# Fifteen tiny loads of 1 to 15 rows, issued between the second and the third piece of the last weight load

## The chip, the cores and the metric

The kernel runs on one core of a Trainium2 chip. The metric is the device time of one execution in microseconds (us); the number that counts is the median over several runs.

## What is computed

One token is decoded through an attention layer with a long cache, a gated feed-forward layer, and a gate that mixes the two:

```python
q = x @ wq                                   # 32 query heads of 128
scores = einsum(q, k) * Dh ** -0.5           # 8 key heads, each for 4 query heads, 32768 positions
p = softmax(scores)
a = einsum(p, v).reshape(B, Sq, Hq * Dh) @ wo    # wo is 4096 x 512
b = (silu(x @ w1) * (x @ w3)) @ w2           # 512 -> 1792 -> 512
g = sigmoid((x * gate_w).sum(-1))
out = g * a + (1 - g) * b
```

All data is float32. Keys and values make up most of what has to be read from memory: 8 x 32768 x 128 numbers each.

## The kernel before

The whole program is written as a list of operations per engine. A small planner (the class `Program`) goes through them in the order of the code, notes who writes and who reads what, and puts the semaphore waits in; each engine then runs its own list in that order. So the order of the code is the order on each engine.

SyncE (SP in the profile) issues all big loads, on one queue (q1 in the profile). `load` (L199) issues one, with a semaphore for that load. Two large buffers, `big_a` and `big_b`, of 128 rows by 16384 numbers each take turns: keys in 8 MB pieces, the query weights first, the values in 8 MB pieces. A load into a buffer waits, on SyncE, for the last reader of what lies in it. TensorE takes the products; VectorE turns the keys; ScalarE copies and takes the exponentials.

At the end stands the part that the change touches. The last four value pieces are loaded by `load_unit` (L199) and used by `values` (TensorE, L574). Behind the last value piece SyncE issues `w2` into the tile `aside`, and then, as soon as TensorE has read the first part of head 7 out of `big_a`, the output weights `wo` into the same buffer, in six pieces whose sizes fall from 4096 KB to 256 KB:

```python
    parts = ((0, 16), (16, 23), (23, 27), (27, 29), (29, 31), (31, 32))
    for a, b in parts:
        load(wo_t[:, a:b, :], wod[:, a:b, :], [("wo", a)], over=["A0", "A1"])
```

Each piece is 128 rows; piece (a, b) has 2048 bytes times (b - a) in a row. TensorE multiplies the first three pieces at L630 (27 slices of 512 columns) and the last three at L661 (in 128 columns each), each when its piece has landed. VectorE then copies the result (L673), SyncE and ScalarE each store half of it (L504), and GpSimd waits for the two stores at the very end.

The tile `kt1`, into which the change loads, is 2048 numbers wide. In its first 1024 columns lies `otp`, the turned attention output that the last products read; the other 1024 columns are not read any more by then.

Of the kernel before, what the change touches and what calls it, by code (L numbers as in the profile page):

```python
# [118 lines left out]
def kernel(  # L119
# [13 lines left out]
    nc = tc.nc  # L133
# [23 lines left out]
    pr = Program(nc, tc.alloc_semaphore)  # L157
# [5 lines left out]
    def sbuf(name, *shape):  # L163
        return nc.alloc_sbuf_tensor(name, [P, *shape], F32)[:]
# [4 lines left out]
    kt = [pool_w[:, NB * 96:NB * 128], sbuf("kt1", NB * 32)]  # L169
# [25 lines left out]
    def load(dst, src, writes, over=()):  # L195
        lanes[0] += 1
        lane = f"load{lanes[0] % 9}"
        return pr.add(
            "SP", lambda: nc.sync.dma_start(dst, src), writes=writes, over=[*over, lane], inc=lane, by=16, also=lane,  # L199
        )  # L200
# [60 lines left out]
    def zeros():  # L261
        return T.matmul(ps_s, acc[:, 0:P], acc, start=True, stop=False, skip_group_check=True)  # L262
# [344 lines left out]
    wod = wo.rearrange("(p k) e -> p k e", k=32)  # L607
    parts = ((0, 16), (16, 23), (23, 27), (27, 29), (29, 31), (31, 32))
    for a, b in parts:
        load(wo_t[:, a:b, :], wod[:, a:b, :], [("wo", a)], over=["A0", "A1"])  # L610


    def spend(bank, n):
# [68 lines left out]
    a, b, c, d = flips  # L682
# [24 lines left out]
    with nc.Fori(0, NH - LAG, 1, engines=[PE], head_slot={PE: 0}):  # L707
# [8 lines left out]
        values_all().then_inc(done, 1)  # L716
        zeros().then_inc(done, 1)
    pr.emit("PE", ops[d:])
    landed = pr.semaphore("stored")
    nc.gpsimd.wait_ge(landed, 32).then_inc(landed, 1)  # L720
    critical.close()
# [28 lines left out]
```

## Time and profile before

| | |
|---|---|
| median of 3 runs | 693.91 us |
| lowest and highest run | 693.82 and 694.04 us |
| profiled execution, from its first to its last instruction | 692.4 us |
| TensorE busy | 402.8 us (58%) |
| VectorE busy | 368.4 us (53%) |
| ScalarE busy | 134.6 us (19%) |
| time of the packets on the load queue, as a share of 16 DMA engines | 99.1% |
| read from memory | 296.23 MB, 428 GB/s over the span |

The profiled execution is known by its span alone: 692.4 us lie between its first and its last instruction. The time of a run is counted from outside, and the median is 1.5 us longer than that span. The engines are a little over half busy at most; the DMA engines, which carry the loads, are busy nearly all the time.

### The profile page before, as it was taken

The numbers are of one execution on the slowest core, as the hardware profiler recorded it, in microseconds if no ns is written. First come the engines' busy times: TensorE is split into PE (matmuls) and PEld (weight loads), VectorE is DVE, ScalarE is ACT, GpSimd is POOL, SyncE is SP. The second block draws the span as 40 slices with busy tenths as digits, with TensorE's granted clock in tenths as the row PEclk, the third lists the DMA queues.
The fourth block names the chain that finished last, engine by engine and source line by source line (L and its number), as shares of the span: only waits on it lengthen the run. The fifth ranks groups of instructions, "written<-read, shape, count | busy, mean of one in ns | idle before, by whom it ended". The sixth has DMA issues, their size and how long they took to land. (4 is left out here: it accounts for less than half of the span.)

```text
span 692.4 us, 5704 instructions
## 1 busy us (share of the span) xinstructions
PE 402.8 (58%) x2430; PEld 94.6 (14%) x2430; DVE 368.4 (53%) x229; ACT 134.6 (19%) x113; POOL 8.1 (1%) x34
## 2 busy tenths in 40 slices
PE   1537777566474656557484645666573646744575
PEld 0101111201010110201010101201010102211121
DVE  0049999394735637493726537593826546700026
ACT  0143223232303130220303131210303131100000
POOL 4000000000000000000000000000000000000000
PEclk9969999958667676977786777778586777776689
DMA  9999999999999999999999999999999999999996
GB/s 386 455 428 424 424 424 436 448 443 424 428 428 428 435 454 432 424 432 428 432 454 435 424 428 428 432 435 451 432 424 428 428 435 454 435 421 424 433 421 284
DMA packets 6068, 296.34 MB, mean 428 GB/s; under 512 B 678, under 2 KB 682, under 8 KB 1068
## 3 DMA queue, kind: packets, MB, share of 16 engines
q1 hardware_dynamic: 6052, 296.23, 99.1%
q8 instruction: 5, 0.08, 0.0%
q14 instruction: 3, 0.02, 0.0%
q10 hardware_dynamic: 8, 0.01, 0.0%
HBM read 296.23 MB, written 0.00 MB: 428 GB/s over the span
## 5 line engine op out<-in xcount | busy, mean ns | idle before, releaser
L366 DVE STREAM_TRANSPOSE aside<-big_a 128x2048 f32<-128x2048 f32 x41 | 94.3, 2300 | 166.9 <-DMA big_a<-in_A_k_cache_dram 166.9
L350 PE MATMUL ps<-aside,winc 128*32 128x512 f32 x512 | 96.0, 830 | 142.4 <-PEq L688 141.5
L350 PE MATMUL ps<-kt,winc 128*32 128x512 f32 x512 | 96.2, 832 | 61.2 <-PEq L688 61.2
L451 PE MATMUL ps<-big_b,pv 128*32 128x512 f32 x768 | 96.1, 657 | 17.5 <-PEq L688 17.5
L338 ACT COPY aside<-big_a 128x6144 f32<-128x6144 f32 x14 | 74.4, 5313 | 151.8 <-DMA big_a<-in_A_k_cache_dram 151.8
L366 DVE STREAM_TRANSPOSE kt<-aside 128x2048 f32<-128x2048 f32 x32 | 73.4, 2293 | 17.2 <-PE ps L350 17.2
L366 DVE STREAM_TRANSPOSE kt<-big_a 128x2048 f32<-128x2048 f32 x28 | 63.5, 2269 | 0.0
L379 ACT COPY sb<-ps 128x512 f32<-128x512 f32 x16 | 17.1, 1069 | 156.8 <-PE ps L350 156.8
L350 PEld LDWEIGHTS ps<-aside,winc 128*32 128x32 f32 x512 | 13.4, 125 | 215.7 <-issue 215.7
L451 PEld LDWEIGHTS ps<-big_b,pv 128*32 128x32 f32 x768 | 27.7, 120 | 88.1 <-issue 88.1
L366 DVE STREAM_TRANSPOSE aside<-aside 128x2048 f32<-128x2048 f32 x16 | 36.3, 2269 | 0.0
L583 DVE TENSOR_TENSOR sb<-ps,own_b 128x512 f32<-128x512 f32 x2 | 1.4, 691 | 60.8 <-PE ps L574 60.8
L350 PEld LDWEIGHTS ps<-kt,winc 128*32 128x32 f32 x512 | 13.3, 123 | 143.8 <-issue 143.8
L574 PE MATMUL ps<-big_b,probs 128*32 128x512 f32 x128 | 18.0, 726 | 18.8 <-DMA big_b<-in_A_v_cache_dram 18.8
L344 ACT COPY winc<-win 128x128 f32<-128x128 f32 x32 | 9.8, 306 | 78.7 <-PE ps L350 78.7
L574 PE MATMUL ps<-big_a,probs 128*32 128x512 f32 x128 | 17.3, 703 | 10.1 <-DMA big_a<-in_A_v_cache_dram 10.1
L614 PE MATMUL ps<-win,ones 128*128 128x512 f32 x42 | 22.7, 635 | 0.0
L366 DVE STREAM_TRANSPOSE aside<-big_b 128x2048 f32<-128x2048 f32 x7 | 16.0, 2291 | 11.4 <-DMA big_b<-in_A_k_cache_dram 11.4
L262 PE MATMUL ps<-acc 128*128 128x512 f32 x34 | 20.0, 670 | 2.5 <-POOL acc L219 1.6
L400 DVE TENSOR_REDUCE mt<-turned 128x8 f32<-128x2048 f32 x4 | 9.2, 2291 | 22.6 <-PE turned L389 22.6
L424 DVE TENSOR_REDUCE sums<-probs 128x8 f32<-128x2048 f32 x4 | 15.2, 3801 | 2.1 <-ACT probs L417 2.1
L288 PE MATMUL turned<-big_a,xp 128*32 128x512 f32 x64 | 8.5, 691 | 12.1 <-DMA big_a<-in_A_wq_dram 12.1
(93 smaller groups left out, 186.6 us busy)
## 6 DMA issues: line engine op xcount, KB each, us to landing
big_b<-in_B_w_dram SPq DMA_DIRECT2D x2, 3584.0 KB, 20.8
big_a<-in_A_wo_dram SPq DMA_DIRECT2D x1, 4096.0 KB, 27.6
aside<-in_B_w_dram SPq DMA_DIRECT2D x1, 3584.0 KB, 37.4
big_a<-in_A_wo_dram SPq DMA_DIRECT2D x1, 1792.0 KB, 31.5
big_a<-in_A_wo_dram SPq DMA_DIRECT2D x1, 1024.0 KB, 33.5
big_a<-in_A_wo_dram SPq DMA_DIRECT2D x2, 512.0 KB, 34.7
big_a<-in_A_wo_dram SPq DMA_DIRECT2D x1, 256.0 KB, 35.2
big_a<-in_A_k_cache_dram SPq DMA_DIRECT2D x14, 26.3
```

Of the source, the lines that this page charges most:

```text
L262: return T.matmul(ps_s, acc[:, 0:P], acc, start=True, stop=False, skip_group_check=True)
L288: ins = T.matmul(pf[b][32 * j:32 * j + 32, :], xp[:, c, :], t[:, o:o + REP * DH], start=(c == 0), stop=(c == NC - 1),)
L338: act(lambda: A.copy(spare, src[:, :, 32:128]), reads=[key], writes=["wo"])
L344: lambda: A.copy(winc, win[:, t // 4, :, 16 - 16 * z:48 - 16 * z]),
L350: ins = T.matmul(ps_s[32 * g:32 * g + 32, :], winc[:, c, :], kt[c % 2][:, 512 * g:512 * g + 512], start=False, stop=False, skip_group_chec ...
L366: k = dve(lambda d=dst, s=src: V.transpose(d, s), reads=[key], writes=[f"kt{c % 2}"], over=["kt0"] * (t >= LAG and (z, c) == (1, 1)), cred ...
L379: lambda: A.copy(sb[:, :, :, t % 4], ps_s.rearrange("p (n i) -> p n i", i=32)),
L400: dve(lambda: V.tensor_reduce(mt[:, 0:8], turned.rearrange("p (n q) -> p q n", q=8), axis=AX.X, op=ALU.max), reads=banks, writes=["mt"])
L424: dve(lambda: V.tensor_reduce(sums[:, 8 * w:8 * w + 8].rearrange("p (u q) -> p u q", u=2), probs[:, :, 0:1024].rearrange("p u (n q) -> p u ...
L451: ins = T.matmul(ps_o[32 * t:32 * t + 32, :], pv[:, o:o + 32], big[1][:, n * P:(n + 4) * P], start=((z, g) == (0, 0)), stop=((z, g) == (1, ...
L574: ins = T.matmul(ps_o[32 * t:32 * t + 32, :], prob[u][:, o:o + 32], vt[:, n * P:(n + 4) * P], start=((e, z, g) == (0, 0, 0)), stop=((e, z, ...
L614: return T.matmul(bank[:, 0:n], ones, win.rearrange("p w c n -> p (w c n)")[:, 0:n], start=True, stop=True)
```

## The change

Between the second and the third piece of `wo`, SyncE issues fifteen more loads. Load n has n rows (n from 1 to 15) of 4 + n numbers (20 to 76 bytes), from the start of the first n rows of the `wo` view, into the unused columns of `kt1`. They all count up one semaphore, `few`, by 16 each. No engine reads what they bring. GpSimd waits for `few` to reach 240, ahead of its last wait.

```diff
     for a, b in parts:
         load(wo_t[:, a:b, :], wod[:, a:b, :], [("wo", a)], over=["A0", "A1"])
+        for n in range(1, 16) if a == 16 else ():
+            pr.add("SP", lambda n=n: nc.sync.dma_start(kt[1][0:n, 1024 + 32 * n:1028 + 33 * n], wod[0:n, 0, 0:4 + n]),
+                   writes=[("few", n)], over=["kt1"], inc="few", by=16)
...
     pr.emit("PE", ops[d:])
+    nc.gpsimd.wait_ge(pr.semaphore("few"), 15 * 16)
     landed = pr.semaphore("stored")
     nc.gpsimd.wait_ge(landed, 32).then_inc(landed, 1)
```

This is what stands on SyncE in the changed kernel around the place, with each instruction's waits (the rows L199 are pieces of `wo`, the rows L612 the new loads into `kt1`):

```order
L199 DMA big_a<-in_A_wo_dram 128x8192 [waits PE]
L199 DMA big_a<-in_A_wo_dram 128x3584
L612 DMA kt<-in_A_wo_dram 1x5
L612 DMA kt<-in_A_wo_dram 2x6
...
L612 DMA kt<-in_A_wo_dram 14x18
L612 DMA kt<-in_A_wo_dram 15x19
L199 DMA big_a<-in_A_wo_dram 128x2048
L199 DMA big_a<-in_A_wo_dram 128x1024 x2
L199 DMA big_a<-in_A_wo_dram 128x512
L504 DMA out_dram<-winc 2x128 [waits DVE]
```

The four last pieces of `wo` have moved behind fifteen issues; the new loads wait for nothing themselves. On GpSimd the difference is in one row, at the end of the program, behind the last tile that it clears:

```order
 L536 MEMSET kt 128x1024 [waits PE]
 L199 UNCONDITIONAL_BRANCH
-L156 UNCONDITIONAL_BRANCH [waits stored]
+L156 UNCONDITIONAL_BRANCH [waits stored,few]
 L156 NO_OP [waits Activation_49]
```

One wait has come in beside the one on the stores; nothing else has moved there.

## Rows read from the trace of the kernel before

**Rows 1.** The page: DMA busy tenths in 40 slices, and the queues (packets, MB, share).

```profile
DMA  9999999999999999999999999999999999999996
q1 hardware_dynamic: 6052, 296.23, 99.1%
q10 hardware_dynamic: 8, 0.01, 0.0%
```

**Rows 2.** The chain that ended last, from 613 us: start, us, what.

```profile
613.04 28.62 DMA big_a<-in_A_v_cache_dram
...
641.79 9.86 PE ps L574 x64
...
651.67 0.33 SPq L199
651.99 0.04 issue
652.04 0.43 SPq L199
652.47 0.04 issue
652.51 0.43 SPq L199
...
653.46 35.07 DMA big_a<-in_A_wo_dram
688.53 0.04 issue
688.58 1.10 PE turned L661 x24
...
689.70 0.29 DVE winc L673
```

**Rows 3.** Issues by line and size: KB each, median us from issue to landing.

```profile
big_a<-in_A_wo_dram SPq DMA_DIRECT2D x1, 4096.0 KB, 27.6
big_a<-in_A_wo_dram SPq DMA_DIRECT2D x1, 1792.0 KB, 31.5
big_a<-in_A_wo_dram SPq DMA_DIRECT2D x1, 1024.0 KB, 33.5
big_a<-in_A_wo_dram SPq DMA_DIRECT2D x2, 512.0 KB, 34.7
big_a<-in_A_wo_dram SPq DMA_DIRECT2D x1, 256.0 KB, 35.2
```

**Rows 4.** Stretches near the end: ..., granted clock, DMA share, GB/s.

```profile
684.00:686.00 2.00, 1.51 (x14) 0.24 (x6) 0.90 (x2) 0.00 (x0) 0.00 (x0) 1.00 1.00 402
686.00:687.00 1.00, 0.92 (x8) 0.16 (x8) 0.00 (x0) 0.00 (x0) 0.00 (x0) 1.00 0.79 305
687.00:688.00 1.00, 0.80 (x24) 0.42 (x23) 0.69 (x1) 0.00 (x0) 0.00 (x0) 1.00 0.37 147
688.00:689.00 1.00, 0.81 (x24) 0.49 (x24) 0.00 (x0) 0.00 (x0) 0.00 (x0) 1.00 0.12 45
```

**Rows 5.** DMA packets of the stretch 690.5 to 691 us (the two stores).

```profile
DMA packets 8, 0.00 MB, mean 4 GB/s; under 512 B 4, under 2 KB 8, under 8 KB 8
...
q1 hardware_dynamic: 4, 0.00, 0.9%
```

**Rows 6.** DMA packets of the stretch 686 to 688.8 us.

```profile
DMA packets 212, 0.50 MB, mean 178 GB/s; under 512 B 33, under 2 KB 33, under 8 KB 212
...
q1 hardware_dynamic: 212, 0.50, 45.6%
```

**Rows 7.** DMA packets of 688.2 to 688.8 us: busy tenths in 40 slices, sums.

```profile
DMA  0307000330003300030000030000300000000000
...
DMA packets 15, 0.02 MB, mean 34 GB/s; under 512 B 5, under 2 KB 5, under 8 KB 15
```

**Rows 8.** Timeline near the end: start, us, instruction [idle before <-releaser].

```profile
687.35 0.64 PE L661 MATMUL turned<-big_a,kt 128*32 128x128 f32 x16 [0.20 <-DMA big_a<-in_A_wo_dram]
...
689.21 0.16 PEld L661 LDWEIGHTS turned<-big_a,kt 128*32 128x32 f32 x8 [0.25 <-DMA big_a<-in_A_wo_dram]
...
690.02 0.33 SPq L504 DMA_DIRECT2D out_dram<-winc  x1
```

**Rows 9.** Queues of the stretch 640 to 693 us.

```profile
q8 instruction: 2, 0.03, 0.3%
```

## The prediction

> **What bounds the kernel now.** I began with the page's slices and queues. The DMA engines are at nine tenths or more in every slice but the last, and the load queue's packets fill 99.1% of the time of sixteen engines [rows 1]. So the kernel is a stream of loads, and what matters is whether the change makes that stream longer or leaves a hole in it.
>
> Next the chain that ended last, for its end. TensorE sets SyncE free at 651.6 us, SyncE issues the pieces of wo one after the other from 651.67 us, and behind the fifth issue stands a transfer of 35.07 us; then come 1.10 us of products at L661, 0.29 us of copying, and the store [rows 2]. The time to landing says why the transfer is so long: the first piece, issued at 651.67, lands after 27.6 us, the third after 33.5, the last after 35.2 [rows 3]. These pieces stand in a queue behind value and w2 loads. The last of them has only 256 KB, which the queue moves in 0.6 us at the 428 GB/s of the table. The issue is not what they wait for.
>
> Last the stretches near the end. From 684 to 686 us the DMA share is 1.00; from 686 to 687 it is 0.79; from 687 to 688 it is 0.37; from 688 to 689 it is 0.12 [rows 4]. A share of 0.37 of sixteen engines is six engines. So the sixteen do not finish together: ten of them have run dry by about 687 us, and six carry the end, the last of them to about 688.7 us (the last slice of 15 ns with work is the 29th from 688.2, so 688.62 and the packet begun in it) [rows 7]. That is 1.7 us of room on ten engines, and little or none on the others.
>
> **The change, part by part.**
>
> *The issues on SyncE.* An issue that waits for nothing takes 0.43 us with 0.04 us behind it [rows 2]. Fifteen take 15 x 0.47 = 7.1 us, if a load of few rows is issued as slowly as one of 128 rows; the store of two rows, with its wait, takes 0.33 us as the first wo piece with its wait does [rows 2, 8], so rows don't seem to matter. The third piece is then issued at 652.5 + 7.1 = 659.6 us instead of 652.51, the last about 661. When do the engines need it? The second piece, issued at 652.04, lands after 31.5 us, so at 683.5 [rows 2, 3]. The engine that is first may be done with it some 2.5 us earlier (I take the spread of the end, from about 686.2, where the share has left 1.00, to 688.7), at about 681. So 21 us of queued data cover a delay of 7.1 us. I cost the issues at nothing. If the cover were gone, all 7.1 us would show. Behind the new issues on SyncE only the four pieces and the store wait; the store is due at 690.02 [rows 8].
>
> *The packets.* How many packets does a load of n rows make? ScalarE's queue q10 had 8 in the whole program [rows 1], for two loads of one row and one store of two rows. This fits one data packet and one semaphore packet for each row: 2 + 2 + 4. The last store shows the same: four packets on q1, two of them under 512 bytes, for two rows, beside ScalarE's four [rows 5]. So the fifteen loads make 120 data packets and 120 semaphore packets. If row number i goes to engine number i, the first engine gets a share of all fifteen loads, the second of fourteen, and the sixteenth of none; on average 7.5.
>
> *What one costs.* No packet of 20 to 76 bytes with its write into the tile is in this trace. From below: the four packets of the store took 0.9% of 16 x 0.5 us, which is 72 ns, or 18 ns each; a pair, data and semaphore, 36 ns [rows 5]. From above: between 686 and 688.8 us 212 packets, of which 33 are semaphores and the rest 2 KB or 4 KB, took 45.6% of 16 x 2.8 us, 20.4 us, so 96 ns each; a pair of such would be 0.19 us [rows 6]. A tiny packet carries a hundredth of that data, so it is nearest to the store, and I take 36 ns. On the engine with all fifteen that is 0.54 us, on an average one 0.27 us. If the engine that ends last is one with room it costs nothing at all. Which engine ends last, no view tells. I choose +0.3 us, the average. At the upper price the first engine would be 15 x 0.19 = 2.9 us late: 2.9 us if it is the last, 1.2 us if it has the room of 1.7 us. The low end is zero; a gain is excluded here, since no byte and no packet goes away.
>
> *What is late next.* The pieces behind the new loads land later by the same fraction of a microsecond. TensorE waits for each of them already [rows 8], so the delay goes through to the products, the copy and the store one for one.
>
> *GpSimd's wait and the write into kt1.* GpSimd waits for `few` where it waits for the stores anyway. The tiny loads stand ahead of the third piece in the queue, so they have landed some microseconds before the stores. Nothing is queued behind this wait but the end. The columns written are read by nobody. Both cost nothing.
>
> *The sum.* Span 692.4 + 0.3 = 692.7 us; the median stands 1.5 us above the span, so 693.91 + 0.3 = **694.2 us**, +0.04%. A difference under 0.2% (1.4 us) can't be told from none in this kernel.
>
> **A rule that speaks against it.** In the trace the three last pieces, each with a semaphore of its own, land at 34.7, 34.7 and 35.2 us after issues half a microsecond apart, and six engines show 0.37 of sixteen, all six busy, while they go from one piece to the next [rows 3, 4]. So between large transfers a queue does not stop for the answer of the one before. The Trainium skill, "DMA: Bandwidth & Descriptors", section "Latency and other measured facts", says that a tiny transfer can't go faster than a round trip to memory of about 800 ns, whatever its size. If each of the fifteen held its engine for that long, an estimate from this page of the Trainium skill is 15 x 0.8 = 12 us; if the round trips overlap, as the trace has it for the pieces, nothing of it shows.
>
> **The rivals.**
>
> *One after the other (slower).* The semaphore packet of a load may have to wait until its data has been answered for, and hold its engine meanwhile. With big packets this is covered, since an engine passes a semaphore only after 0.65 us of data or more (eight packets of 2 KB at 83 ns, from 147 GB/s over 5.9 engines [rows 4]); fifteen loads of one packet each leave no cover. The nearest price is the time from the last packet, at 688.7, to the product that it sets free, at 689.21 [rows 7, 8]: 0.5 us. Fifteen times that are 7.5 us on the first engine: 701.4 us where it is among the six late ones, 699.7 where it has 1.7 us of room. It decides from 0.1 us per load if the first engine ends last (1.4 / 15), and from 0.2 us if it has the room. For it speaks that nothing in the trace has semaphores so close; against it, that no stop is seen at any semaphore so far. The rule of the Trainium skill named above would make this case.
>
> *The issue is late (slower).* If a load of few rows took SyncE over 21 / 15 = 1.4 us instead of 0.47, the queue would run dry ahead of the third piece. At 2 us each it would be 30 - 21 = 9 us: 703 us. Nothing speaks for it: the two-row store was issued in 0.33 us.
>
> *Instructions.* The instruction queue moved two packets in the last 53 us, at 0.3% of 16 x 53 us, so 1.3 us each [rows 9]. They run on the same engines. Fifteen more instructions on SyncE could bring one more, or move one to another engine: up to 1.3 us later where it meets the last engine, 695.2 us, or up to 1.3 us earlier, 692.6 us, where it leaves it. Either way at the edge of what can be told.
>
> *It does not do what it says.* The loads have no reader, but a count that GpSimd waits for; they run. I give this no chance.
>
> **How the numbers follow.** Forecast, tiny packets overlap and cost 0 to 1.4 us: 0.74 (its own range 693.7 to 695.2). One after the other, with over 0.1 us a load: 0.17. Issue late: 0.02. Instructions: 0.07, of which 0.02 end later and 0.02 end earlier by just over 0.2%. Within 0.2% hold the forecast and the rest of the instructions' case, 0.74 + 0.03 = 0.77; slower 0.17 + 0.02 + 0.02 = 0.21; faster 0.02. The range: the upper price of the packets gives 693.9 + 2.9 = 696.8, which also takes in the mild end of the rival with 0.2 us a load; below, half a microsecond under the median for the instructions' case, 693.4. It leaves out the strong rivals, under 0.2.
>
> **What would show it.** Right: fifteen more issues on SyncE of about 0.4 us each between 652.5 and 660 us; 240 more packets on q1; the wo pieces after the second landing within 0.6 us of their old times, counted from the span's start; DMA share 1.00 up to 684 us. Wrong: a DMA share below 1.00 before 684 us with the issues not yet done (SyncE late); one to six engines that carry on for microseconds after the rest, the last piece landing at 695 or later (one after the other); another count of packets on q8 (instructions).

## The result: 0.26% slower

The changed kernel takes 695.75 us (median of 7 runs, 695.35 to 696.25), the kernel before 693.82 us (7 runs beside it, 693.74 to 694.04). The ratio is 1.0026, with a 95% interval from 1.0016 to 1.0035: 1.9 us more. The profiled execution took 695.88 us, 694.1 of them as its span.

The page of the changed kernel shows a queue as full as before, with 240 packets more (6292 for 6052 [rows 1]):

```profile
DMA  9999999999999999999999999999999999999996
q1 hardware_dynamic: 6292, 296.23, 99.0%
q8 instruction: 5, 0.08, 0.0%
q10 hardware_dynamic: 8, 0.01, 0.0%
```

The instruction queue (q8) has the same five packets as before; that fifteen more instructions cost nothing by themselves is shown further down, by the loads behind the last piece. Next SyncE, in its timeline near the end (start, us, instruction, times):

```profile
651.42 0.80 SPq L199 DMA_DIRECT2D big_a<-in_A_wo_dram  x2
652.26 5.27 SPq L612 DMA_DIRECT2D kt<-in_A_wo_dram  x15
657.58 12.27 SPq L199 DMA_DIRECT2D big_a<-in_A_wo_dram  x4
```

Fifteen issues in 5.27 us, where I had 7.1; then four issues that take 12.27 us in place of the 1.9 that four such issues would take. The last of them alone takes 9.2 us. Is the queue starved? Issue and landing, by size, say no:

```profile
big_a<-in_A_wo_dram SPq DMA_DIRECT2D x1, 1792.0 KB, 31.5
big_a<-in_A_wo_dram SPq DMA_DIRECT2D x1, 1024.0 KB, 29.7
big_a<-in_A_wo_dram SPq DMA_DIRECT2D x2, 512.0 KB, 30.9
big_a<-in_A_wo_dram SPq DMA_DIRECT2D x1, 256.0 KB, 29.8
```

The last piece is issued at 669.8 us at the latest and lands 19 us or more after that (its 29.8 us count from when SyncE took it up). Compare the second piece with the third: before, they landed at 652.04 + 31.5 = 683.5 and 652.51 + 33.5 = 686.0 [rows 2, 3]; now at 651.79 + 31.5 = 683.3 and 657.58 + 29.7 = 687.3. The distance has grown from 2.5 to 4.0 us. That is where 1.5 us come in: behind the tiny loads, in the third piece. (The second piece itself lands 0.2 us earlier here than before, so the span of the profiled execution grows by 0.2 us less than the parts below add up to.)

The timeline of TensorE and VectorE near the end (start, us, instruction [idle before <-releaser]) shows the rest:

```profile
683.35 1.92 PE L633 MATMUL turned<-big_a,kt 128*32 128x512 f32 x14 [0.58 <-DMA big_a<-in_A_wo_dram]
687.36 1.27 PE L633 MATMUL turned<-big_a,kt 128*32 128x512 f32 x8 [2.09 <-DMA big_a<-in_A_wo_dram]
688.60 1.08 PE L664 MATMUL turned<-big_a,kt 128*32 128x128 f32 x16
689.88 1.51 PE L664 MATMUL turned<-big_a,kt 128*32 128x128 f32 x24
691.45 0.29 DVE L676 COPY winc<-turned 128x128 f32<-128x128 f32 x1 [2.09 <-PE turned L664]
```

TensorE sat idle for 2.09 us ahead of the third piece. The last 24 products took 1.51 us, before 1.10 [rows 2]. The stretches (us, busy of TensorE, of its weight load, VectorE, ScalarE, GpSimd, granted clock, DMA share, GB/s) show two things:

```profile
684.00:686.00 2.00, 1.27 (x10) 0.12 (x3) 0.65 (x1) 0.00 (x0) 0.00 (x0) 1.00 0.98 368
686.00:687.00 1.00, 0.00 (x0) 0.00 (x0) 0.00 (x0) 0.00 (x0) 0.00 (x0) 1.00 0.94 377
687.00:688.00 1.00, 0.65 (x8) 0.16 (x8) 0.00 (x0) 0.00 (x0) 0.00 (x0) 1.00 0.70 283
688.00:689.00 1.00, 1.00 (x12) 0.39 (x12) 0.33 (x1) 0.00 (x0) 0.00 (x0) 0.54 0.39 154
689.00:690.00 1.00, 1.00 (x28) 0.60 (x22) 0.36 (x1) 0.00 (x0) 0.00 (x0) 0.50 0.12 45
690.00:691.00 1.00, 1.00 (x28) 0.87 (x20) 0.00 (x0) 0.00 (x0) 0.00 (x0) 0.50 0.00 0
```

The DMA shares of 0.70, 0.39 and 0.12 are those of before (0.79, 0.37, 0.12 [rows 4]), one microsecond and a little more later. The granted clock, 1.00 to the end before [rows 4], is 0.54 and 0.50 from 688 us: the lower of its two levels, 1.2 GHz. Half the clock makes the last products 0.4 us longer. 1.5 + 0.4 = 1.9 us is the loss.

**What the tiny packets did.** The trace holds each packet of the queue with its start, size and time, though not its engine. Loads of 1 to 15 rows mark the engines: load n has n packets of a size of its own, and the packets of one engine follow each other without a gap. So the engine that carried all fifteen, the one that carried fourteen, and so on can be told apart, and what came behind on each. This is worked out from the packet records (eight packets of 8192 bytes of the third piece follow on each engine, 309 ns each when nothing holds them). In one place, behind fifteen loads, two packets begin in the same nanosecond; there I take the sequence that every engine with fifteen loads shows in the experiments below.

```
tiny loads  first packet  fourth  fifth   all eight, over 8 x 309
on engine   behind, ns    ns      ns      ns
15          1714          451     814     2060
13          1280          358     821     1549
12          1138          426     818     1471
10           827          534     869     1315
 8           458          588     893     1021
 7           315          309     780      477
 5           316          309     456      154
 4           309          314     309       27
 3           314          309     309        5
```

The tiny packets themselves cost next to nothing: 9 to 12 ns each, 13 ns from one load to the next on an engine, 0.2 us for fifteen. But behind them the engine stops. With four loads or fewer there is no stop; with five to seven it is in the fifth packet, from eight on also in the first and fourth, and it grows to 2.1 us with fifteen. The engine that ended last in the whole kernel is the one with twelve loads, so number 3 if rows are dealt out to engines in order from number 0: from the end of its part of the second piece to its last semaphore it took 7.2 us. The engine that ended last before took 5.7 us for the same stretch. That is the 1.5 us.

The rest of the work is to find out whether this stop is the cause, on which engine it counts, what sets it off, and whether the clock is a part of its own. Every time below is a median; the kernel before, run beside them on the same chip, stood at 693.87, 693.99 and 693.91 us in the three groups. The changed kernel itself was not run again in them.

### The profile page after: what moved, and what is told of

Its sections match the earlier page's. It is cut to its first block, busy times and chain, and to the rows that moved or that the text cites. A ratio compares the mean times of both kernels' runs of the same rounds, so it can differ in the third digit from the quotient of the medians.

```text
span 694.1 us, 5719 instructions
## 1 busy us (share of the span) xinstructions
PE 398.1 (57%) x2430; PEld 94.9 (14%) x2430; DVE 368.3 (53%) x229; ACT 134.6 (19%) x113; POOL 8.1 (1%) x34
## 3 DMA queue, kind: packets, MB, share of 16 engines
q1 hardware_dynamic: 6292, 296.23, 99.0%
## 5 line engine op out<-in xcount | busy, mean ns | idle before, releaser
L350 PE MATMUL ps<-kt,winc 128*32 128x512 f32 x512 | 93.4, 809 | 61.8 <-PEq L691 61.8
L451 PE MATMUL ps<-big_b,pv 128*32 128x512 f32 x768 | 94.2, 647 | 17.5 <-PEq L691 17.5
## 6 DMA issues: line engine op xcount, KB each, us to landing
big_a<-in_A_wo_dram SPq DMA_DIRECT2D x1, 1792.0 KB, 31.5
big_a<-in_A_wo_dram SPq DMA_DIRECT2D x1, 1024.0 KB, 29.7
big_a<-in_A_wo_dram SPq DMA_DIRECT2D x1, 256.0 KB, 29.8
```

Of the source, the lines that this page charges most:

```text
L350: ins = T.matmul(ps_s[32 * g:32 * g + 32, :], winc[:, c, :], kt[c % 2][:, 512 * g:512 * g + 512], start=False, stop=False, skip_group_chec ...
L451: ins = T.matmul(ps_o[32 * t:32 * t + 32, :], pv[:, o:o + 32], big[1][:, n * P:(n + 4) * P], start=((z, g) == (0, 0)), stop=((z, g) == (1, ...
```

## Experiments

### Three rows, four rows

The fifteen loads keep their lengths, 20 to 76 bytes a row, but have three rows each, or four:

```diff
-            pr.add("SP", lambda n=n: nc.sync.dma_start(kt[1][0:n, 1024 + 32 * n:1028 + 33 * n], wod[0:n, 0, 0:4 + n]),
+            pr.add("SP", lambda n=n: nc.sync.dma_start(kt[1][0:3, 1024 + 32 * n:1028 + 33 * n], wod[0:3, 0, 0:4 + n]),
```

> Fifteen loads of 3 rows each (20 to 76 bytes a row) in place of 1 to 15 rows. Theory A (each load holds up only the DMA engine that carries one of its rows, and the end is late only because the engine that ends last, which by the changed kernel's trace carried twelve of the loads and so is number 3, is among them): only the three engines with numbers 0 to 2 are held up, which have 1.3 to 2.1 us of room before the last; each loses about 1.9 us, so the end moves by 0 to 0.6 us: 693.8 to 694.4 us. Theory B (the cost lies in the fifteen issues, in SyncE's blocked queue or in the fifteen semaphores, whoever carries the rows): as the changed kernel, 695.4 to 696.2 us.

> Fifteen loads of 4 rows each. Theory A: engine 3 now carries fifteen loads in place of twelve, loses 1.9 us in place of 1.6, and the TensorE clock falls before the end as in the changed kernel: 695.8 to 696.6 us. Theory B: as the changed kernel and as three rows, 695.4 to 696.2 us. The two theories are told apart by four rows against three: 1.5 to 2 us by A, nothing by B.

Measured: three rows 694.52 us (ratio 1.0008, 0.9999 to 1.0017), four rows 696.28 us (1.0032, 1.0020 to 1.0044). One more row in each load costs 1.8 us, with the same number of loads, issues and semaphores. Theory B falls; A stands, though three rows came in 0.1 us above its range. The packet records show three engines with a first packet of 1.61 to 1.71 us in the one, four with 1.60 to 1.66 us in the other. The lines of TensorE and VectorE, first with three rows:

```profile
687.74 0.64 PE L664 MATMUL turned<-big_a,kt 128*32 128x128 f32 x16 [0.18 <-DMA big_a<-in_A_wo_dram]
689.02 1.03 PE L664 MATMUL turned<-big_a,kt 128*32 128x128 f32 x24 [0.22 <-DMA big_a<-in_A_wo_dram]
690.12 0.29 DVE L676 COPY winc<-turned 128x128 f32<-128x128 f32 x1 [1.80 <-PE turned L664]
```

then with four:

```profile
687.81 1.11 PE L633 MATMUL turned<-big_a,kt 128*32 128x512 f32 x8 [2.02 <-DMA big_a<-in_A_wo_dram]
690.34 1.51 PE L664 MATMUL turned<-big_a,kt 128*32 128x128 f32 x24
691.91 0.29 DVE L676 COPY winc<-turned 128x128 f32<-128x128 f32 x1 [2.25 <-PE turned L664]
```

With three rows the products run at full speed (1.03 us) and wait for landings in between. With four, TensorE idles 2.02 us, and its last products take 1.51 us, as in the changed kernel.

### The same loads behind the last piece

```diff
-        for n in range(1, 16) if a == 16 else ():
+        for n in range(1, 16) if a == 31 else ():
```

> The same fifteen loads of 1 to 15 rows, issued behind the last piece of wo in place of between the second and third. All instructions, packets and waits of the change are there, but no piece stands behind them in the queue. Theory A: the pieces land as in the kernel before, only the result's store comes behind the loads, with over a microsecond between: 693.7 to 694.3 us. If the presence of the instructions, of the packets or of the wait at the end costs by itself: up to 695.8 us.

Measured: 694.00 us (1.0002, 0.9993 to 1.0011). All the packets, instructions and waits of the change are there, and nothing is lost. SyncE's timeline is the more telling:

```profile
650.13 2.70 SPq L199 DMA_DIRECT2D big_a<-in_A_wo_dram  x6
652.88 23.89 SPq L612 DMA_DIRECT2D kt<-in_A_wo_dram  x15
689.84 0.25 SPq L504 DMA_DIRECT2D out_dram<-winc  x1
```

SyncE spends 23.89 us in the issues of the tiny loads, where 5.27 were enough in the changed kernel, and the kernel is as fast as before, since SyncE has nothing else to do until 689.84. So an issue can be held, and this by itself costs nothing while the queue has work. The run also has all fifteen extra instructions of the change, so these cost nothing either.

### One load with fifteen runs in each row

```diff
-        for n in range(1, 16) if a == 16 else ():
-            pr.add("SP", lambda n=n: nc.sync.dma_start(kt[1][0:n, 1024 + 32 * n:1028 + 33 * n], wod[0:n, 0, 0:4 + n]),
-                   writes=[("few", n)], over=["kt1"], inc="few", by=16)
+        if a == 16:
+            pr.add("SP", lambda: nc.sync.dma_start(
+                kt[1][0:16, 1024:2048].rearrange("p (n i) -> p n i", i=64)[:, 0:15, 0:12], wod[0:16, 0:15, 0:12],
+            ), writes=[("few", 0)], over=["kt1"], inc="few", by=16)
...
-    nc.gpsimd.wait_ge(pr.semaphore("few"), 15 * 16)
+    nc.gpsimd.wait_ge(pr.semaphore("few"), 16)
```

> One load in place of fifteen: 16 rows with fifteen runs of 12 numbers (48 bytes) in each, so each of the sixteen engines gets fifteen tiny data packets and one semaphore packet. If the price is per tiny data packet, every engine loses about 1.9 us and the end is as late as with four rows, 695.8 to 696.6 us. If the price hangs on the semaphore packets or on separate loads, only one of fifteen is paid, which is covered: 693.8 to 694.3 us.

Measured: 694.17 us (1.0006, 0.9996 to 1.0015). The range of the second case. Fifteen tiny data packets on every engine, with one semaphore packet behind them, made no single long stop: by the packet records those of the third piece took 2.8 us longer in all, 0.18 us on an average engine. So the 1.5 us are not the price of tiny data packets. They belong to fifteen loads, each with its own semaphore packet; whether to the semaphore packets or to the loads being separate, this run does not tell, since one cannot be had without the other. Here too SyncE was held, with one load in place of fifteen:

```profile
651.52 10.30 SPq L199 DMA_DIRECT2D big_a<-in_A_wo_dram  x4
```

So a held issue goes without the loss in this run as well.

### Other data: from the chip, and from other addresses

The loads read from the identity tile on the chip, or each from an address of its own:

```diff
-            pr.add("SP", lambda n=n: nc.sync.dma_start(kt[1][0:n, 1024 + 32 * n:1028 + 33 * n], wod[0:n, 0, 0:4 + n]),
+            pr.add("SP", lambda n=n: nc.sync.dma_start(kt[1][0:n, 1024 + 32 * n:1028 + 33 * n], ident[0:n, 0:4 + n]),
...
+            pr.add("SP", lambda n=n: nc.sync.dma_start(kt[1][0:n, 1024 + 32 * n:1028 + 33 * n], wod[0:n, 2 * n, 0:4 + n]),
```

> The same fifteen loads of 1 to 15 rows, but each reads its rows out of the on-chip identity tile in place of the weights in memory; the rest is the changed kernel. If the stop of 0.8 us in the first packet after the twelve loads on engine 3 comes from the way to memory of each tiny read, it goes, and the time is 693.8 to 694.3 us. If it comes from handling a load with a semaphore of its own, wherever its data lies: 695.4 to 696.2 us.

> The same fifteen loads, but load n reads its rows 4096 bytes times n further on, so that no two loads read the same address. If the fifteen reads of one address in memory stand in each other's way, the stops go: 693.8 to 694.3 us. If the address is nothing to it: 695.4 to 696.2 us.

Measured: from the chip 696.04 us (1.0029, 1.0018 to 1.0040), from other addresses 695.43 us (1.0022, 1.0013 to 1.0032). Neither takes the stop away. The first packet behind twelve loads took 1.40 us in the one and 1.13 in the other, in the changed kernel 1.14; the packets of the third piece were late by 13.6, 12.6 and 12.5 us over all engines. So it is not the way to memory of a tiny read, nor the shared address that is read. The second kernel's profiled execution kept its clock, and its last products took 1.05 us.

### Seven loads of sixteen rows

```diff
-        for n in range(1, 16) if a == 16 else ():
-            pr.add("SP", lambda n=n: nc.sync.dma_start(kt[1][0:n, 1024 + 32 * n:1028 + 33 * n], wod[0:n, 0, 0:4 + n]),
+        for n in range(1, 8) if a == 16 else ():
+            pr.add("SP", lambda n=n: nc.sync.dma_start(kt[1][0:16, 1024 + 32 * n:1028 + 33 * n], wod[0:16, 0, 0:4 + n]),
...
-    nc.gpsimd.wait_ge(pr.semaphore("few"), 15 * 16)
+    nc.gpsimd.wait_ge(pr.semaphore("few"), 7 * 16)
```

> Seven loads of 16 rows in place of fifteen of 1 to 15, so seven on every engine. In the changed kernel's trace an engine that carried seven loads or fewer shows no longer first packet after them, and each load over seven adds about 0.18 us to it. If so, seven are covered also on the engine that ends last: 693.8 to 694.4 us. If every load costs the same, at 1.6 us for twelve: 0.9 us and perhaps the lower clock, 694.8 to 695.3 us.

Measured: 694.55 us (1.0007, 0.9998 to 1.0016). A miss between the two: I had read only the first packet in the table and not the fourth and fifth. The stop in the first packet is gone with seven, as read; the second is there, 0.6 us an engine (9.45 us over sixteen), and the end is late by 0.56 us. By the timeline of SyncE no issue is held here:

```profile
655.70 1.84 SPq L199 DMA_DIRECT2D big_a<-in_A_wo_dram  x4
```

Set beside the one load with fifteen runs, this run says more. There an engine passed 16 packets (15 of data, one semaphore) and lost 0.18 us behind them, with an issue held; here it passed 14 packets (seven of each) and lost 0.6 us, with none held. So the stop follows neither the number of tiny packets nor the hold on SyncE.

### Three groups of five

Fifteen loads of four rows, but five behind the second piece, five behind the third and five behind the fourth:

```diff
-        for n in range(1, 16) if a == 16 else ():
+        for n in {16: range(1, 6), 23: range(6, 11), 27: range(11, 16)}.get(a, ()):
```

> Fifteen loads of 4 rows, in three groups of five: behind the second, the third and the fourth piece. If an engine stops only where more than about five tiny loads follow each other (in the changed kernel's trace the engine with five lost 0.15 us, that with fifteen 1.7 us), engine 3 loses about 0.2 us at each group at most and the clock stays: 694.0 to 694.7 us. If every load has its price of 0.12 us wherever it stands: as the fifteen loads of 4 rows in one place, 695.9 to 696.4 us.

Measured: 694.51 us (1.0006, 0.9997 to 1.0015), against 696.28 us with the same fifteen loads in one place. The price is not one per load; it grows with the number that follow each other. By the packet records the first group held the fifth packet of the third piece for 0.14 to 0.24 us; at the head of the third group the semaphore ahead of it and its first tiny packet took 0.13 to 0.18 us longer, and the first packet of the sixth piece 0.12 to 0.17 us; the middle group held nothing. With the 0.2 us that fifteen tiny loads take themselves this is some 0.7 us on one engine, where the kernel lost 0.6.

### Between the first and the second piece

```diff
-        for n in range(1, 16) if a == 16 else ():
+        for n in range(1, 16) if b == 16 else ():
```

with four rows in each load, as above.

> Fifteen loads of 4 rows between the first and the second piece, so with packets of 14336 bytes behind them in place of 8192. If the stop belongs to the loads, whatever follows, engine 3 loses the same 1.8 us; the end is late by that, and the clock may fall or not: 695.4 to 696.4 us. If it needs the smaller packets behind it: 694.0 to 695.0 us.

Measured: 695.94 us (1.0027, 1.0017 to 1.0036). Behind the loads now stand packets of 14336 bytes, which take 540 ns; on four engines the first took 1.84 to 1.89 us and a later one 1.08 to 1.14, so 1.9 us in all on each, as behind the second piece. The stop belongs to the loads, not to what follows. In the profiled execution the clock kept its level here, and from the second piece on TensorE waited for no landing longer than 0.58 us.

### Every engine with fifteen

```diff
-            pr.add("SP", lambda n=n: nc.sync.dma_start(kt[1][0:n, 1024 + 32 * n:1028 + 33 * n], wod[0:n, 0, 0:4 + n]),
+            pr.add("SP", lambda n=n: nc.sync.dma_start(kt[1][0:16, 1024 + 32 * n:1028 + 33 * n], wod[0:16, 0, 0:4 + n]),
```

> Fifteen loads of 16 rows at the place of the change: 240 data packets in place of 60 with four rows, every engine with fifteen. If only the engine that ends last counts, it has the same fifteen loads as with four rows: 695.9 to 696.6 us. If the number of packets or of engines that stop counts, it is a microsecond or more later than with four rows: over 697 us.

Measured: 696.65 us (1.0035, 1.0023 to 1.0047), a hair above the first range and clear of the second. Four times as many engines stop (34 us over all engines, against 7.6 with four rows), and the time moves by 0.4 us. But the two profiled executions differ in their clock too (two lines of the timeline, then a stretch in the columns above):

```profile
688.51 1.06 PE L633 MATMUL turned<-big_a,kt 128*32 128x512 f32 x8 [2.74 <-DMA big_a<-in_A_wo_dram]
691.01 1.06 PE L664 MATMUL turned<-big_a,kt 128*32 128x128 f32 x24 [0.19 <-DMA big_a<-in_A_wo_dram]
689.00:690.00 1.00, 0.82 (x16) 0.24 (x12) 0.35 (x1) 0.00 (x0) 0.00 (x0) 1.00 0.39 156
```

The clock stayed at 1.00 here, and the last products took 1.06 us against 1.51 with four rows. The products of the third piece begin at 688.51 us, with four rows at 687.81. So the transfers are 0.7 us later than with four rows, and the higher clock gives some of it back. The engine that ends last decides most of the loss; how the stops of the others add to it is not taken apart.

### Idle products against the fall of the clock

```diff
     for i, (a, b) in enumerate(parts[:3]):
+        for _ in range(5) if i == 2 else ():
+            idle_product(512)
```

> The changed kernel with five idle products of 512 columns on TensorE ahead of the products of the third piece; they compute nothing that is used. In the changed kernel TensorE is idle from 685.3 to 687.4 us, its granted clock is 0.50 from 688.5 us on, and from the last landing to the copy it takes 1.4 us in place of 1.0. If the lower clock is a part of the loss, it stays at 1.00 here and about 0.4 us come back: 695.2 to 695.5 us. If the clock costs nothing there, because the last landing decides alone: 695.6 to 696.0 us.

Measured: 698.17 us (1.0057, 1.0043 to 1.0070). A mis-sized experiment. An idle product of this size is two passes of 0.46 us, and five of them took 4.56 us where the gap had 2, so the third piece waited for them. The run tells nothing on the size of the clock's part. So again, with one:

```diff
     for i, (a, b) in enumerate(parts[:3]):
+        if i == 2:
+            idle_product(512)
```

> The changed kernel with one idle product (two passes of 0.46 us) ahead of the products of the third piece, in place of the five that held the third piece up by 3 us. TensorE's gap of 2.1 us becomes two of about 1.2 us or less. If the lower clock at the end is a part of the loss, it stays at 1.00 in every run, the runs lie closer together, and the median is 0.3 to 0.5 us under the changed kernel's: 695.2 to 695.5 us. If it costs nothing: 695.6 to 696.0 us.

Measured: 695.44 us (1.0021, 1.0012 to 1.0030), ten of eleven runs between 695.12 and 695.56 us. The changed kernel's own runs lie between 695.35 and 696.25. In the trace the gap is split, and the products keep their speed:

```profile
685.14 1.13 PE L617 MATMUL ps<-win,ones 128*128 128x512 f32 x2
687.09 1.06 PE L633 MATMUL turned<-big_a,kt 128*32 128x512 f32 x8 [0.82 <-DMA big_a<-in_A_wo_dram]
689.58 1.06 PE L666 MATMUL turned<-big_a,kt 128*32 128x128 f32 x24 [0.19 <-DMA big_a<-in_A_wo_dram]
690.70 0.29 DVE L678 COPY winc<-turned 128x128 f32<-128x128 f32 x1 [1.79 <-PE turned L666]
```

The stretches of the same kernel, in the columns above, at the same place as in the changed kernel:

```profile
688.00:689.00 1.00, 0.83 (x24) 0.41 (x22) 0.69 (x1) 0.00 (x0) 0.00 (x0) 1.00 0.38 147
689.00:690.00 1.00, 0.81 (x24) 0.49 (x24) 0.00 (x0) 0.00 (x0) 0.00 (x0) 1.00 0.07 27
```

The clock is 1.00 where it was 0.54 and 0.50, and the last products take 1.06 us in place of 1.51. So the clock's fall is a part of its own, 0.4 us in an execution in which it falls. The medians agree, with an excess over the kernel before of 1.5 us in place of 1.9, but they were not taken side by side and their intervals overlap. Nor is it shown that the idle product kept the clock up: with sixteen rows in each load TensorE sat idle for 2.74 us and the clock kept its level, while behind waits of 2.09 us (the changed kernel) and 2.02 (four rows) it fell. The kernel with other addresses kept it too, so it does not seem to fall in every execution; what sets it off stays open.

## Why the prediction was right and where it was wrong

*The bound.* Right. The kernel is a stream of loads, and only what delays the last engine of the sixteen counts. That six engines carry the end and ten have room stands in the packet records of the kernel before: ten have ended by 687.05 us, six end from 688.06 to 688.72. Three rows against four showed what it means: three engines with room, held up by 1.9 us each, cost 0.65 us; with the fourth, on which the kernel then ends, it is 2.4 us, 0.4 of them by the clock.

*The issues on SyncE at nothing.* Right, with two wrong sizes: 5.27 us in place of 7.1, since rows do matter (0.23 us for two, 0.38 for fifteen), and two later issues that took 11 us, which I had not thought of. Both stayed under the cover. With the loads behind the last piece SyncE spent 24 us on them, and the time was that of before.

*The number of packets.* Right: 240, with the shares of fifteen, fourteen and so on.

*What one costs.* This step failed. "I take 36 ns" for a pair of packets; the pair takes 13 ns, so even that was too much, but the packets behind it stop. Nor did the average engine decide, which I had chosen, but one of the six late ones. On the engine that ended last, twelve loads cost 1.5 us, 0.13 us a load, within my upper price of 0.19 us and over three times what I took. The trace before did not show it: between two semaphores of one engine on the load queue stand the packets of a whole piece there. I looked for the price of a packet in the packet's own time, and it stood in the time of the next ones.

*The rival "one after the other".* It had the right form, an engine held because loads without cover follow each other, and the right bound: it decides from 0.1 us a load if a held engine ends last. Its price of 0.5 us a load was four times too high, and the mechanism is milder than I put it: up to four loads in a row are free, fifteen in a row hold their engine for 1.8 to 2.1 us, and three groups of five cost 0.6 us. Nor does the engine stop at the semaphores, as I had it: they take 9 ns each, and the stop is in the large packets that follow. The rule of the Trainium skill quoted with it ("DMA: Bandwidth & Descriptors", "Latency and other measured facts"), that no tiny transfer is faster than a round trip to memory of some 800 ns, does not add up load by load here: an engine passes fifteen in 0.2 us. And reading from the chip in place of memory, 696.04 us, did not help.

*What is late next.* Half right. The delay goes through to the products one for one, but I left out that TensorE's clock can fall. That is 0.4 us of the 1.9, in the executions in which it happens. And of the signs that I had named for being right one failed: the pieces behind the second were to land within 0.6 us of their old times, and the third landed at 687.3 in place of 686.0.

*The rival "instructions".* The count of the instruction packets did not change, and the same fifteen instructions behind the last piece cost nothing. This rival was out.

So the time lay within the range, at 695.75 for a forecast of 694.2, but with six times the added time that I had forecast and by another mechanism. In part that is luck: the range went up to 696.8 by a price taken from packets of 2 and 4 KB and by the mild end of a rival to which I had given 0.17, and not by the stop that the runs showed. The difference from before is by its middle value just over the 0.2% that I had put as the bound; its interval, 0.16 to 0.35%, holds that bound.

**What stays open.** Whether the semaphore packets or the separate loads make the engine stop; the one large load with fifteen runs has only one of each. All fifteen loads count up one and the same semaphore, and loads with a semaphore each were not run. Why the stop comes in two parts, in the first and in the fourth and fifth packet. What holds an issue on SyncE, and what makes the clock fall behind one wait and not behind another. That the engines are numbered by rows from 0 is an inference from the packet counts; nothing depends on the numbers.

## What to carry to other kernels

Where a kernel is a stream of loads, look at how the sixteen DMA engines end, not at their mean: a delay on an engine with room is free as far as the room goes, the same delay on the last one counts in full. Many tiny loads in a row cost less by their own packets than by the stop behind them; four in a row on an engine cost nothing here, twelve 1.5 us; put them behind the last large load (0.1 us here), spread them in small groups (0.6 us for what cost 2.4 in one place), or make one load of many runs (0.3 us). And when a landing is late near the end, look at the granted clock behind the longer wait before the whole loss is put down to the transfer.

## What the runs showed of the hardware

An issue on SyncE takes 0.23 us for a load of two rows and 0.38 for one of fifteen, and it can be held: for 9.2 us at the sixth piece here, and for 1.0 to 2.4 us at one tiny load after another, from the third on, where they stood last. With seven loads of sixteen rows no issue was held, with one load of fifteen runs one was. A tiny data packet takes 9 to 12 ns, and an engine passes a load of one tiny packet with its semaphore every 13 ns. A stop behind fifteen such loads is 1.8 to 2.1 us, in the packets that follow, whether these have 8192 or 14336 bytes, and whether the tiny loads read memory or the chip. An instruction packet takes one of the same engines: while one was under way (646.67 to 647.74 us in the kernel before), fifteen packets of the load queue were in flight in place of sixteen.
